# Loading two weight matrices in row groups of 2, 2, 4, 8 and 120 partitions instead of whole, in a decode kernel that streams a KV cache

## The chip, the cores and the metric

The kernel runs on one core of one Trainium2 chip. The metric is the device time of one execution in microseconds (us), lower is better. Executions of one kernel agree within about 0.25% here.

PE is the matrix engine, DVE the vector engine, ACT the scalar engine, SP the engine whose sequencer issues nearly all loads. The loads themselves are moved by 16 DMA engines, which are called "transfer engines" below. The trace shows a load as packets, which one engine moves one after another (their times are in the table below). A load has landed when all its engines have counted up its semaphore, and whoever waits for the load goes on then: in the kernel before the semaphore of the first V block has 16 arrivals, the last at 61.89 us, and PE starts on the block at 61.93 us.

## The reference

One token passes through attention over a long cache and through a gated feed-forward block, and a scalar gate mixes the two:

```python
q = (x @ wq)                                  # 32 heads of 128, x is 512 wide
scores = einsum(q, k_cache) * 128 ** -0.5     # 65,536 keys per head, bf16
a = (softmax(scores) @ v_cache) @ wo
b = (silu(x @ w_gate) * (x @ w_up)) @ w_down      # the same x
g = sigmoid((x * gate_w).sum())
return g * a + (1 - g) * b
# (cut: shapes, transposes, input setup)
```

The K and V caches have 1,074 MB together. All weights together have about 14 MB. gate and up, which the change touches, are 512 x 1792 in bf16: 1.8 MB each, 0.3% of the traffic together.

## The kernel before

On-chip memory holds three slots of 8 MB. K and V blocks of 8 MB go through them in turn. wq, gate and up share slot 0 at the start; the first K block goes to slot 1 and the first V block to slot 2. SP issues, in this order, wq, four pieces of the first K block, gate, up, the first V block. The next K block may be issued when the feed-forward matmuls have read gate and up.

```python
def dma(key, out_ap, in_ap, writes=(), reads=(), sem=None, engine="SP"):
    op(engine, key, lambda: emit[engine].dma_start(out=out_ap, in_=in_ap),
       reads=reads, writes=writes, sem=sem or key)
# ...
dma("wq", wq_sb, A_wq.rearrange("(p t) f -> p t f", t=KT), units(0, 0, WQ))
# ...
load("k", 0, [EK] * (KPP // EK))              # first K block, four pieces
G0, U0 = WQ, WQ + KT * F
gate_v, up_v = view(0, G0, KT, F), view(0, U0, KT, F)
dma("gate", gate_v, B_w_gate.rearrange("(p t) f -> p t f", t=KT), units(0, G0, U0))
dma("up", up_v, B_w_up.rearrange("(p t) f -> p t f", t=KT), units(0, U0, U0 + KT * F))
load("v", 0, [KPP])                           # first V block
# ...
def hidden():                                 # the feed-forward matmuls
    # ... 112 matmuls over gate_v and up_v
    group("gu", parts, units(0, G0, U0 + KT * F) + ["Xc"], ["m_x"])
```

Each partition receives one row of gate, 4 x 1792 x 2 = 14,336 contiguous bytes, as one packet. "Row" means this below.

The softmax here doesn't subtract the row's maximum and nothing guards it: scores larger than these inputs give would overflow.

Of the kernel before, what the change touches and what calls it, by code (L numbers as in the profile page):

```python
# [79 lines left out]
def kernel(  # L80
# [20 lines left out]
    F = B_w_gate.shape[1]  # L101
    KT = D // P
# [14 lines left out]
    def sb(name, shape, dtype):  # L117
        return consts.tile(shape, dtype, name=name)
# [11 lines left out]
    Xc = sb("Xc", [P, KT], bf16)  # L130
# [27 lines left out]
    m_x = psum.tile([P, 512], f32, name="m_x")  # L158
# [7 lines left out]
    def op(engine, key, fn, reads=(), writes=(), sem=None):  # L166
        plan.add(engine, key, fn, list(reads), list(writes), sem)

    def units(s, a, b):

        w = UNIT * Dh
        return [(s, u) for u in range(a // w, -(-b // w))]

    def view(s, a, t, n):
        return slot[s][:, a : a + t * n].rearrange("p (t n) -> p t n", t=t)

    def dma(key, out_ap, in_ap, writes=(), reads=(), sem=None, engine="SP"):
        op(
            engine, key, lambda: emit[engine].dma_start(out=out_ap, in_=in_ap),
            reads=reads, writes=writes, sem=sem or key,  # L180
        )
# [16 lines left out]
    def load(which, n, pieces):  # L198
        cache = A_k_cache if which == "k" else A_v_cache
        h, c = divmod(n, CH)  # L200
        s = where[which, n] = take()
        src = cache[0, h, c * P * KPP : (c + 1) * P * KPP, :].rearrange(
            "(p j) d -> p j d", j=KPP
        )
        t = view(s, 0, KPP, Dh)
        at = 0
        for m in pieces:
            dma(
                (which, n, at), t[:, at : at + m, :], src[:, at : at + m, :],
                units(s, at * Dh, (at + m) * Dh),  # L210
                sem=f"slot{s}" if len(pieces) == 1 else f"{which}{n}_{at}",
            )
            at += m
        assert at == KPP

    load("k", 0, [EK] * (KPP // EK))
    G0, U0 = WQ, WQ + KT * F
    gate_v, up_v = view(0, G0, KT, F), view(0, U0, KT, F)
    dma("gate", gate_v, B_w_gate.rearrange("(p t) f -> p t f", t=KT), units(0, G0, U0))
    dma("up", up_v, B_w_up.rearrange("(p t) f -> p t f", t=KT), units(0, U0, U0 + KT * F))  # L220
    load("v", 0, [KPP])


# [35 lines left out]
    def group(key, parts, reads, writes):  # L259


        def fn():
            for out_ap, pairs in parts:
                for i, (a, b) in enumerate(pairs):
                    ins = nc.tensor.matmul(  # L265
                        out_ap, lhsT=a, rhs=b, start=(i == 0), stop=(i == len(pairs) - 1)
                    )
            return ins

        op("PE", key, fn, reads, writes)  # L270

    def act(key, out_ap, in_ap, func, reads, writes, **kw):
        op(
            "ACT", key, lambda: nc.scalar.activation(out=out_ap, in_=in_ap, func=func, **kw),  # L274
            reads, writes,
        )

    def dve(key, fn, reads, writes):
        op("DVE", key, fn, reads, writes)
# [117 lines left out]
    def hidden():  # L397
        parts = []
        for w, wv in enumerate((gate_v, up_v)):
            for ft in range(FT):  # L400
                parts.append(
                    (
                        m_x[:, w * FT + ft : w * FT + ft + 1],
                        [(wv[:, t, bass.ds(ft, P, FT)], Xc[:, t : t + 1]) for t in range(KT)],
                    )
                )
        group("gu", parts, units(0, G0, U0 + KT * F) + ["Xc"], ["m_x"])
        act("gu_sb", gu_sb, m_x[:, : 2 * FT], ACT.Copy, ["m_x"], ["gu_sb"])
        act("eg", eg, gu_sb[:, :FT], ACT.Exp, ["gu_sb"], ["eg"], scale=-1.0)
        dve("eg1", lambda: nc.vector.tensor_scalar_add(eg, eg, 1.0), ["eg"], ["eg"])  # L410
        dve("eg2", lambda: nc.vector.reciprocal(eg, eg), ["eg"], ["eg"])
        dve(
            "eg3",
            lambda: nc.vector.tensor_tensor(out=eg, in0=gu_sb[:, :FT], in1=eg, op=ALU.mult),
            ["eg", "gu_sb"], ["eg"],
        )
        dve(
            "hT",
            lambda: nc.vector.tensor_tensor(out=hT, in0=eg, in1=gu_sb[:, FT:], op=ALU.mult),
            ["eg", "gu_sb"], ["hT"],  # L420
        )
# [79 lines left out]
    for n in range(N - 1):  # L501
        h, c = divmod(n, CH)
        if c == 0:
            cut[h] = len(plan.ops)
        if n:
            load("k", n, [KPP])
            load("v", n, [KPP])
        m = HK if n else EK
        for j in range(0, KPP, m):
            block(n, j, m)  # L510
            if j == 0:
                if c == 0 and h + 1 < H:
                    spread(h + 1)
                if pending:
                    diagonal()
            elif n == N - 2:
                norm(0, H - 1)
                outputs()
            while len(todo) > 1:
                gather()  # L520
        gather()
        if n == 0:
            gate()
            hidden()
        if n == N - 2:
            turn_outputs(0)
        pv(n)
# [35 lines left out]
    at = 0  # L563
# [27 lines left out]
    with tc.tile_critical():  # L591
        sems = {}
        for o in plan.ops:
            for s in [o.token[0], *o.waits]:
                if s not in sems:
                    name = "s_" + "".join(ch if ch.isalnum() else "_" for ch in str(s))
# [66 lines left out]
```

## Time and profile before

| | kernel before |
|---|---|
| time | 2522.36 us, median of 2 runs (2521.55 to 2523.16) |
| busy | PE 79%, DVE 50%, ACT 4% of the span |
| load queue | 99.7% of the span of 16 transfer engines |
| rate in the middle | 433 to 436 GB/s |
| one 65,536-byte packet | 2418 ns, the next begins about 4 ns before its end |
| one 14,336-byte packet | 535 ns, all 256 of gate and up alike |

The first view is the profile's page of the kernel before. "busy tenths" cuts the span in 40 slices; the line DMA is the busy share of the transfer engines, GB/s what they moved. The last line is the load queue: packets, bytes, share of 16 engines' span.

```profile
PE 1979.0 (79%) x9115; PEld 823.1 (33%) x9115; DVE 1268.4 (50%) x286; ACT 97.4 (4%) x398; POOL 1.9 (0%) x9
...
DMA  9999999999999999999999999999999999999998
GB/s 423 430 432 433 435 433 434 434 435 436 435 435 434 433 434 435 434 434 434 435 436 434 435 433 434 434 435 435 434 433 435 436 435 435 433 433 434 436 429 359
...
q1 hardware_dynamic: 20880, 1087.78, 99.7%
```

The transfer engines are busy all the time, the compute engines are not. The packet records of the trace say the same per engine: a 65,536-byte packet takes 2418 ns (15,959 of 16,000 to the nanosecond), so one engine moves 27.1 GB/s and 16 of them 434 GB/s. This fixed pace is the limit.

The next view lists issues: what is loaded, how often, KB each, and us from issue to landing.

```profile
slot_65<-in_B_w_gate_dram SPq DMA_DIRECT2D x1, 1792.0 KB, 34.9
slot_65<-in_B_w_up_dram SPq DMA_DIRECT2D x1, 1792.0 KB, 38.6
...
slot_67<-in_A_k_cache_dram SPq DMA_DIRECT2D x21, 35.9
```

An 8 MB block takes 19.3 us at 434 GB/s but lands 35.9 us after its issue: every engine has work queued ahead.

The chain of waits is the work that ended last, followed back from the end: start, duration, what. First its pieces near the start, then those near the end.

```profile
45.07 6.85 PE m_x L265 x112
51.92 9.96 another core or an unknown queue
61.93 16.00 PE O_ps L251 x64
77.94 41.90 DMA slot_67<-in_A_k_cache_dram
```

```profile
2390.83 13.99 PE O_ps L251 x64
...
2404.83 34.67 DMA slot_67<-in_A_k_cache_dram
...
2439.53 8.70 DVE slot_67 L324
```

At 45.07 us PE begins the 112 feed-forward matmuls; gate and up had landed at 38.4 and 42.6 us by the issues above. "another core or an unknown queue" at 51.92 is PE's wait for the first V block; the timeline names it as the load of V into slot 2 and shows PE starting on it at 61.93 us. Near the end, the last full K block lands at 2439.50 us, and some 80 us of PE and DVE work follow that hardly wait for loads any more. Therefore a microsecond added to the engine that finishes last should move the end by about a microsecond.

The last view of before divides the stretch in which gate and up are loaded into windows of 5 us. Columns: window, its length, busy us (instructions) of PE, PEld, DVE, ACT, POOL, then granted clock, DMA share and GB/s. A share over 1 shows that packets are not cut exactly at a window's edges.

```profile
core 0: us, PE busy (x) PEld busy (x) DVE busy (x) ACT busy (x) POOL busy (x), PEclk, DMA share, GB/s
33.00:38.00 5.00, 3.59 (x16) 1.49 (x16) 5.00 (x3) 0.35 (x2) 0.00 (x0) 1.00 0.99 422
38.00:43.00 5.00, 3.66 (x17) 1.49 (x16) 1.88 (x2) 0.35 (x2) 0.00 (x0) 1.00 1.20 517
43.00:48.00 5.00, 3.30 (x51) 3.25 (x52) 1.76 (x6) 0.52 (x3) 0.00 (x0) 0.76 1.12 485
48.00:53.00 5.00, 3.92 (x66) 3.84 (x64) 0.50 (x3) 0.41 (x2) 0.00 (x0) 0.50 1.02 436
```

The rate stays above 420 GB/s through all of it.

### The profile page before, as it was taken

How to read it: one execution, taken by the hardware profiler on the slowest of the kernel's cores; microseconds unless marked ns; L12 is line 12 of the kernel's file. 1: busy time of each engine (PE TensorE's matmuls, PEld its weight loads, DVE VectorE, ACT ScalarE, POOL GpSimd, SP SyncE). 2: the span in 40 equal slices, each digit the busy share in tenths (PEclk: the TensorE clock that was granted, in tenths of full speed). 3: DMA queues.
4: the chain of work that ended last, by engine and by line, in shares of the span. 5: the costliest groups of instructions: out<-in, count | busy, mean ns of one | idle time of the engine just before them, and what ended most of it. 6: DMA issues, size and time to landing. Idle time of an engine off the chain costs nothing.

```text
span 2520.2 us, 19415 instructions
## 1 busy us (share of the span) xinstructions
PE 1979.0 (79%) x9115; PEld 823.1 (33%) x9115; DVE 1268.4 (50%) x286; ACT 97.4 (4%) x398; POOL 1.9 (0%) x9
## 2 busy tenths in 40 slices
PE   4787877877778778778787787787787877877878
PEld 2233332333333333333333333333333332333334
DVE  3455355464553554644645546446455455464553
ACT  0000000000000000000000000000000000000000
POOL 0000000000000000000000000000000000000000
PEclk8888988989889899899898898998998988989888
DMA  9999999999999999999999999999999999999998
GB/s 423 430 432 433 435 433 434 434 435 436 435 435 434 433 434 435 434 434 434 435 436 434 435 433 434 434 435 435 434 433 435 436 435 435 433 433 434 436 429 359
DMA packets 20906, 1088.09 MB, mean 432 GB/s; under 512 B 2450, under 2 KB 2580, under 8 KB 2836
## 3 DMA queue, kind: packets, MB, share of 16 engines
q1 hardware_dynamic: 20880, 1087.78, 99.7%
q8 instruction: 16, 0.26, 0.0%
q14 instruction: 6, 0.05, 0.0%
q10 hardware_dynamic: 4, 0.00, 0.0%
HBM read 1087.77 MB, written 0.00 MB: 432 GB/s over the span
## 4 chain that ended last, share of the span: by engine, by line
DMA 44%; PE 41%; DVE 13%; ACT 1%; another core or an unknown queue 0%; issue 0%; SPq 0%; DVEq 0%; ACTq 0%
PE O_ps L251 18%; DMA slot_67<-in_A_k_cache_dram 16%; DMA slot_66<-in_A_k_cache_dram 14%; DMA slot_65<-in_A_k_cache_dram 14%; PE S_ps_101 L265 12%; PE S_ps_102 L265 9%; DVE slot_66 L324 4%; DVE slot_67 L324 4%; DVE slot_65 L324 3%; DVE S_sb_82 L349 2%; PE m_c L251 2%; PE m_x L265 1%; ACT P_sb_83 L274 1%; DMA slot_65<-in_A_wq_dram 0%
## 5 line engine op out<-in xcount | busy, mean ns | idle before, releaser
L265 PE MATMUL S_ps_101<-slot_67,ident 128*128 128x512 bf16 x704 | 204.1, 462 | 134.5 <-DVE slot_67 L324 134.5
L265 PE MATMUL S_ps_101<-slot_66,ident 128*128 128x512 bf16 x672 | 196.6, 464 | 128.3 <-DVE slot_66 L324 128.3
L265 PE MATMUL S_ps_101<-slot_65,ident 128*128 128x512 bf16 x672 | 189.6, 452 | 132.6 <-DVE slot_65 L324 132.6
L324 DVE TENSOR_TENSOR slot_67<-slot_67,q_bc_79 128x16384 bf16<-128x16384 bf16 (+1 forms) x26 | 207.9, 8033 | 142.0 <-DMA slot_67<-in_A_k_cache_dram 142.0
L349 DVE TENSOR_REDUCE S_sb_82<-S_ps_102 128x128 f32<-128x1024 f32 (+1 forms) x66 | 78.7, 1192 | 387.9 <-PE S_ps_102 L265 387.9
L324 DVE TENSOR_TENSOR slot_65<-slot_65,q_bc_78 128x16384 bf16<-128x16384 bf16 x22 | 190.2, 8689 | 145.7 <-DMA slot_65<-in_A_k_cache_dram 145.7
L324 DVE TENSOR_TENSOR slot_66<-slot_66,q_bc_78 128x16384 bf16<-128x16384 bf16 (+1 forms) x24 | 190.6, 7977 | 136.1 <-DMA slot_66<-in_A_k_cache_dram 120.4
L324 DVE TENSOR_TENSOR slot_67<-slot_67,q_bc_78 128x16384 bf16<-128x16384 bf16 x20 | 172.9, 8689 | 121.9 <-DMA slot_67<-in_A_k_cache_dram 121.9
L324 DVE TENSOR_TENSOR slot_66<-slot_66,q_bc_79 128x16384 bf16<-128x16384 bf16 x20 | 172.9, 8688 | 118.7 <-DMA slot_66<-in_A_k_cache_dram 118.7
L324 DVE TENSOR_TENSOR slot_65<-slot_65,q_bc_79 128x16384 bf16<-128x16384 bf16 x20 | 172.9, 8689 | 118.5 <-DMA slot_65<-in_A_k_cache_dram 118.5
L251 PE MATMUL O_ps<-slot_67,P_sb_83 128*4 128x512 bf16 x704 | 155.7, 382 | 28.3 <-ACT P_sb_83 L274 18.3
L251 PE MATMUL O_ps<-slot_65,P_sb_83 128*4 128x512 bf16 x704 | 155.2, 381 | 20.7 <-ACT P_sb_83 L274 20.7
L251 PE MATMUL O_ps<-slot_66,P_sb_84 128*4 128x512 bf16 x704 | 153.7, 379 | 19.3 <-ACT P_sb_84 L274 19.3
L265 PEld LDWEIGHTS S_ps_101<-slot_67,ident 128*128 128x128 bf16 x704 | 79.1, 115 | 258.9 <-DVE slot_67 L324 145.1
L265 PEld LDWEIGHTS S_ps_101<-slot_66,ident 128*128 128x128 bf16 x672 | 75.7, 116 | 249.1 <-DVE slot_66 L324 139.0
L265 PE MATMUL S_ps_102<-slot_67,ident 128*128 128x512 bf16 x704 | 155.9, 379 | 0.2 <-DVE slot_67 L324 0.2
L265 PEld LDWEIGHTS S_ps_101<-slot_65,ident 128*128 128x128 bf16 x672 | 74.1, 113 | 248.4 <-DVE slot_65 L324 143.2
L251 PE MATMUL O_ps<-slot_65,P_sb_84 128*4 128x512 bf16 x640 | 139.7, 379 | 18.3 <-ACT P_sb_84 L274 18.3
L251 PE MATMUL O_ps<-slot_67,P_sb_84 128*4 128x512 bf16 x640 | 139.7, 379 | 18.3 <-ACT P_sb_84 L274 18.3
L251 PE MATMUL O_ps<-slot_66,P_sb_83 128*4 128x512 bf16 x640 | 139.7, 379 | 17.5 <-ACT P_sb_83 L274 17.5
L265 PE MATMUL S_ps_102<-slot_66,ident 128*128 128x512 bf16 x672 | 148.7, 379 | 1.3 <-DVE slot_66 L324 1.3
L265 PE MATMUL S_ps_102<-slot_65,ident 128*128 128x512 bf16 x672 | 148.6, 379 | 0.1
(83 smaller groups left out, 860.1 us busy)
## 6 DMA issues: line engine op xcount, KB each, us to landing
slot_66<-in_A_k_cache_dram SPq DMA_DIRECT2D x4, 2048.0 KB, 24.7
slot_67<-in_A_k_cache_dram SPq DMA_DIRECT2D x4, 2048.0 KB, 23.9
slot_65<-in_A_wq_dram SPq DMA_DIRECT2D x1, 4096.0 KB, 12.3
slot_66<-in_A_wo_dram SPq DMA_DIRECT2D x1, 4096.0 KB, 30.7
slot_65<-in_A_v_cache_dram SPq DMA_DIRECT2D x1, 4096.0 KB, 17.6
slot_65<-in_A_v_cache_dram SPq DMA_DIRECT2D x1, 2048.0 KB, 22.1
slot_65<-in_B_w_gate_dram SPq DMA_DIRECT2D x1, 1792.0 KB, 34.9
slot_65<-in_B_w_up_dram SPq DMA_DIRECT2D x1, 1792.0 KB, 38.6
```

Source lines behind the costliest of these rows:

```text
L251: ins = nc.tensor.matmul(out_ap, lhsT=a, rhs=b, start=start and i == 0, stop=stop and i == len(pairs) - 1,)
L265: ins = nc.tensor.matmul(out_ap, lhsT=a, rhs=b, start=(i == 0), stop=(i == len(pairs) - 1))
L274: "ACT", key, lambda: nc.scalar.activation(out=out_ap, in_=in_ap, func=func, **kw),
L324: "products", lambda: nc.vector.tensor_tensor(out=w, in0=w, in1=q_rep, op=ALU.mult),
L349: lambda: nc.vector.tensor_reduce(out=S_sb[b][:, :m], in_=S_ps[r][:, :m, :], axis=AXIS.X, op=ALU.add),
```

## The change

It makes the load uneven over the transfer engines: gate is loaded as 8 and 120 rows, up as 2, 2, 4 and 120. No byte and no matmul is added. The group of matmuls waits for six loads instead of two.

```diff
-    dma("gate", gate_v, B_w_gate.rearrange("(p t) f -> p t f", t=KT), units(0, G0, U0))
-    dma("up", up_v, B_w_up.rearrange("(p t) f -> p t f", t=KT), units(0, U0, U0 + KT * F))
+    for name, w_v, w, a, b, parts in (
+        ("gate", gate_v, B_w_gate, G0, U0, [8, 120]),
+        ("up", up_v, B_w_up, U0, U0 + KT * F, [2, 2, 4, 120]),
+    ):
+        at = 0
+        for m in parts:
+            dma(
+                f"{name}{at}", w_v[at : at + m], w.rearrange("(p t) f -> p t f", t=KT)[at : at + m],
+                [(*u, name, at) for u in units(0, a, b)],
+            )
+            at += m
# ... and the group "gu" reads the names of all six pieces
```

More of the change, by code (lines that the diff above doesn't have):

```diff
@@ L406, in hidden @@
                 )
-        group("gu", parts, units(0, G0, U0 + KT * F) + ["Xc"], ["m_x"])
+        group(
+            "gu", parts,
+            units(0, G0, U0 + KT * F) + ["Xc"]
+            + [(*u, "gate", at) for u in units(0, G0, U0) for at in (0, 8)]
+            + [(*u, "up", at) for u in units(0, U0, U0 + KT * F) for at in (0, 2, 4, 8)],
+            ["m_x"],
+        )
         act("gu_sb", gu_sb, m_x[:, : 2 * FT], ACT.Copy, ["m_x"], ["gu_sb"])
```

## The prediction

> **What bounds it now.** The transfers. The page's slices show the DMA engines busy at 90% or more everywhere and some 434 GB/s; the queue table gives the load queue 99.7% of 16 engines' span for 1087.78 MB. The trace's packet records show why: every 65,536-byte packet takes 2418 ns and the next starts about 4 ns before its end, so each engine runs at a fixed 27.1 GB/s. PE is busy 79%, DVE 50%. Steady K loads are issued about 36 us before they land (DMA issues view), although 8 MB takes only 19.4 us: every engine has queued work. In the timeline the last full K load lands at 2439.5 us; some 80 us of PE and DVE work follow, with 2 to 3 us of slack against the last loads. So a microsecond added to the slowest engine's queue is a microsecond of the total.
>
> **What changes.** No byte, no matmul; two loads become six. [...] A row is 14,336 bytes, 535 ns in the trace. Rows per engine, before: 16 everywhere (8.5 us). After: engines 0 and 1 get 20, 2 and 3 get 18, 4 to 7 get 17, 8 to 14 get 16, engine 15 none. Costs:
>
> 1. Four rows more on engines 0 and 1: +2.1 us (estimate, 4 x 0.53). Engine 15's 8.5 us lead buys nothing: each slot waits for all engines. The 16 landings of one load spread over 0.7 us early and 3.4 us late, in steps of 1.2 us (single pauses of an engine), so part may hide: +1 to +2.1.
> 2. Port conflicts. [...] Likelier than not, at partial strength.
> 3. Four more issues on SP at 0.45 to 0.5 us: free, the queue is 28 us deep then. Four more waits on PE: nothing.
>
> On the critical path: 1 and 2 in full. Gate and up land at 38.4 and 42.6 us; PE uses them at 45.07, and the first V load behind them lands at 61.9. A delay to about 55 us only starts the next issue later, with the queue still full.
>
> **Predicted:** 2529 us (+7), 2522.5 to 2537. Faster by over 2%: 0.5%; within 2%: 99%; slower by over 2%: 0.5%.
>
> **What would show it.** Right: the V load's landing and every later one shift by the total's change; 14,336-byte packets take longer than 535 ns (step 2); the 16 landings of a later load spread over about 10 us, one engine far ahead (step 1); steady packets stay at 2418 ns. Step 2 wrong: those packets stay at 535 ns and the total rises 1 to 2 us.
>
> **What would make it wrong.** A different split of 120 rows [...]; the slow engines being those without extra rows (+0); a queue running dry.

The sizes of term 2: up to +4.2 us for each 120-row load (8 packets at half the pace, 8 x 0.53 us), +8.5 us for both, and +1 to +4 us for the small loads. These were estimates, on the assumption that engines which write to certain partitions at the same time share the pace of one. The sum of +7 us is +1 to +2.1 us from term 1, and the rest from term 2 taken "at partial strength"; term 3 adds nothing. The rows per engine were a forecast too; the profile after shows the counts. The packet records name no engine.

## The result, and the profile after

| | before | after |
|---|---|---|
| time | 2522.36 us (2521.55 to 2523.16) | 2534.28 us (2532.76 to 2535.79) |
| runs | 2 | 2 |
| ratio of fast runs | | 1.0047, 95% interval 1.0023 to 1.0072 |

A ratio is the mean time of one kernel's fast runs over that of the other's in the same rounds, so it is not quite the ratio of the medians quoted. The change costs 11.9 us: far less than 2%, but clear of the noise.

The page after, the same lines:

```profile
PE 1979.0 (78%) x9115; PEld 823.1 (32%) x9115; DVE 1268.2 (50%) x286; ACT 97.3 (4%) x398; POOL 1.9 (0%) x9
...
DMA  9999999999999999999999999999999999999998
GB/s 339 431 436 433 436 432 432 437 432 436 432 437 432 436 432 436 434 435 432 435 433 434 436 432 434 437 434 432 433 437 436 432 433 434 437 432 432 436 428 347
...
q1 hardware_dynamic: 20894, 1087.78, 99.6%
```

PE's busy time is the same to the last digit. The two executions that were profiled differ by 13.9 us in their spans (2520.2 to 2534.1), a little more than the medians. Of the 40 rates, the first fell from 423 to 339 GB/s, a fifth of a slice of 63 us, 12 to 13 us; the last fell from 359 to 347, the others are as before (431 to 437 in the middle). So nearly the whole cost arises in the first 63 us.

The issues after; the small groups (112, 28 and 56 KB) have no landing time in this view, so only the two large ones are shown:

```profile
slot_65<-in_B_w_gate_dram SPq DMA_DIRECT2D x1, 1680.0 KB, 41.2
slot_65<-in_B_w_up_dram SPq DMA_DIRECT2D x1, 1680.0 KB, 49.8
...
slot_67<-in_A_k_cache_dram SPq DMA_DIRECT2D x21, 36.0
```

The large part of up lands 49.8 us after its issue, where the whole of it took 38.6. A steady K block takes 36.0 against 35.9: the steady loads run as before.

The chain of waits after, near the start and near the end:

```profile
5.25 49.80 DMA slot_65<-in_B_w_up_dram
55.30 6.85 PE m_x L274 x112
62.15 12.52 another core or an unknown queue
74.71 16.67 PE O_ps L260 x64
91.40 41.17 DMA slot_67<-in_A_k_cache_dram
```

```profile
2402.56 13.99 PE O_ps L260 x64
...
2416.56 35.66 DMA slot_67<-in_A_k_cache_dram
...
2452.24 8.70 DVE slot_67 L333
```

PE now waits for up until 55.05 us. It starts on the first V block 12.8 us later than before (74.71 against 61.93), and the last full K block lands 12.7 us later (2452.22 against 2439.50). The tail behind it is the same work (1.2 us longer in this execution, 0.7 of it in one group of PE matmuls). So the delay of the first stage arrives at the end almost whole: 12.7 of the 13.9 us between these two executions.

The same windows after:

```profile
core 0: us, PE busy (x) PEld busy (x) DVE busy (x) ACT busy (x) POOL busy (x), PEclk, DMA share, GB/s
33.00:38.00 5.00, 3.39 (x17) 1.47 (x16) 3.72 (x3) 0.35 (x2) 0.00 (x0) 1.00 0.98 200
38.00:43.00 5.00, 2.32 (x12) 0.97 (x11) 3.52 (x2) 0.35 (x2) 0.00 (x0) 1.00 0.90 181
43.00:48.00 5.00, 1.98 (x10) 0.81 (x8) 1.75 (x6) 0.52 (x3) 0.00 (x0) 1.00 1.02 222
48.00:53.00 5.00, 0.00 (x0) 0.00 (x0) 0.00 (x0) 0.00 (x0) 0.00 (x0) 0.65 1.28 284
```

While gate and up are loaded the rate falls to 181 to 222 GB/s, half of before, and the transfer engines count as busy all the time: they are not idle, they are slow. The packet records show it directly. They name no engine; I linked each packet to the one that starts within nanoseconds of its end, which gives one row per engine (a few links are uncertain). The numbers are ns per 14,336-byte packet, in order:

```
before, any engine, 16 packets:   535 535 535 535 535 535 535 535 535 535 535 535 535 535 535 535
after, engine with 20 packets:    1484 1055 1089 1135 1079 1125 1107 1135 1104 1040 1009 1119 980 952 1185 1179 1136 1049 1047 964
after, engine with 16 packets:    1411 1113 1076 1126 1081 1121 1108 1125 1089 1059 1004 1138 994 946 1152 1193
after, another engine with 16:    1574 1032 1104 1138 1073 1514 1595 1620 1224 1151 1052 942 1100 1501 1607 1626
after, engine with none, first V packets (65,536 bytes, 2418 before):   5285 6614 4904 6021
```

The unevenness is as predicted: some engines have 20 rows, some 18, some 17, some 16, one none. In the trace, the semaphores of the groups of 8, 2, 2 and 4 rows have 9, 3, 3 and 5 arrivals: one at the issue (at 4.0 to 5.4 us, long before the first of these rows moves at 31.8 us), then 8, 2, 2 and 4, as many as there are rows. That of a 120-row group has 16: one at the issue and 15. This fits 8, 2, 2, 4 and 15 engines.

But two things go beyond the prediction. Every engine with rows is slowed to about half (0.93 to 1.3 us for most packets, 535 ns before); this trace alone does not say whether an engine is slowed only by those that write to certain partitions or by any. And the engine that has no row of gate or up, and so began on V early, needs 4.9 to 6.6 us for packets that take 2.4.

Two engines take 1.5 to 1.64 us for two or three packets in a row from 38 us on, and again from 48 us on (one of the two is printed, in the fourth row of numbers). In this time the engine without rows is writing V. Of the packets of the other engines between 38 and 41.5 us, none takes more than 1,139 ns. So whatever slowed these two further did not slow the others; why it was these two is not shown.

### The profile page after: what moved, and what is told of

It is laid out like the page before. It is cut to its first block, busy times and chain, and to the rows that moved or that the text cites. A ratio compares the mean times of both kernels' runs of the same rounds, so it can differ in the third digit from the quotient of the medians.

```text
span 2534.1 us, 19421 instructions
## 1 busy us (share of the span) xinstructions
PE 1979.0 (78%) x9115; PEld 823.1 (32%) x9115; DVE 1268.2 (50%) x286; ACT 97.3 (4%) x398; POOL 1.9 (0%) x9
## 4 chain that ended last, share of the span: by engine, by line
DMA 46%; PE 40%; DVE 12%; ACT 1%; another core or an unknown queue 0%; issue 0%; SPq 0%; DVEq 0%
PE O_ps L260 18%; DMA slot_67<-in_A_k_cache_dram 16%; DMA slot_65<-in_A_k_cache_dram 14%; DMA slot_66<-in_A_k_cache_dram 14%; PE S_ps_101 L274 12%; PE S_ps_102 L274 9%; DVE slot_67 L333 4%; DVE slot_65 L333 3%; DVE slot_66 L333 3%; DMA slot_65<-in_B_w_up_dram 2%; DVE S_sb_82 L358 2%; PE m_c L260 1%; PE m_x L274 1%; ACT P_sb_83 L283 1%
```

## The experiments

Theories, as they stood:

- **Rows.** The fullest engine has 4 rows more, 4 x 0.53 = 2.1 us, and everybody waits for it.
- **Ports.** "Port" is whatever engines share that write to neighbouring partitions at the same time. Two such engines would take about twice 535 ns for a packet, four about four times (estimates, by an even share); the theory took two for 64-row loads and four for 16-row loads. Loads over all 128 partitions would stay as they are (535 ns in the kernel before). In the prediction only the engines that crowd each other were slow. No trace had shown this when the expectations were written.
- **Rivals.** A fixed cost for each load; a weakness of loads that use fewer than 16 engines; a slow reading side (neighbouring rows in memory).

Every kernel below gave the right result and was timed in 5 rounds beside the kernel before, whose medians were 2522.49, 2522.60 and 2522.97 us in the three groups. Differences are those of medians.

### Even, on part of the partitions: two loads of 64 rows, eight loads of 16

```diff
-        ("gate", gate_v, B_w_gate, G0, U0, [8, 120]),
-        ("up", up_v, B_w_up, U0, U0 + KT * F, [2, 2, 4, 120]),
+        ("gate", gate_v, B_w_gate, G0, U0, [64, 64]),             # second kernel: [16] * 8
+        ("up", up_v, B_w_up, U0, U0 + KT * F, [64, 64]),          # second kernel: [16] * 8
```

> Gate and up each as two loads of 64 rows: all 16 engines get the same number of rows (4 per load, 16 in all)[...]. Port theory: 14,336-byte packets about 1,050 ns instead of 535, first V load about 8.4 us later, total +8.4 us (2530.8), landings of a V load as close together as before (under 1 us). Uneven-load theory (only the extra rows of the fullest engine cost): no engine has more rows, so +0. Theory that groups of fewer than 16 engines or odd group sizes are slow: +0.[...]

> Gate and up each as eight loads of 16 rows, one row per engine and load: even again[...]. Port theory: packets about 2,100 ns, total +25 us (2547.7). Uneven-load theory: +0. Theory that each additional load costs a fixed time (14 more loads here, 4 more in the change and +11.9 us there): +42 us.

With 64-row loads: 2531.46 us (+9.0, as the port theory expected with +8.4), ratio 1.0037 (1.0023 to 1.0051). With 16-row loads: 2540.48 us (+18.0), ratio 1.0072 (1.0058 to 1.0085). The windows of the two, 64 rows first:

```profile
core 0: us, PE busy (x) PEld busy (x) DVE busy (x) ACT busy (x) POOL busy (x), PEclk, DMA share, GB/s
33.00:38.00 5.00, 3.63 (x16) 1.49 (x16) 3.70 (x3) 0.35 (x2) 0.00 (x0) 1.00 0.98 210
38.00:43.00 5.00, 2.79 (x9) 1.11 (x10) 2.76 (x2) 0.35 (x2) 0.00 (x0) 0.82 1.03 218
```

```profile
core 0: us, PE busy (x) PEld busy (x) DVE busy (x) ACT busy (x) POOL busy (x), PEclk, DMA share, GB/s
33.00:38.00 5.00, 3.57 (x16) 1.47 (x16) 2.30 (x3) 0.35 (x2) 0.00 (x0) 1.00 0.98 132
38.00:43.00 5.00, 0.90 (x4) 0.30 (x4) 4.70 (x2) 0.27 (x2) 0.00 (x0) 0.90 1.02 138
```

All 16 engines are at work at about one pace in both (the DMA share, taken over 16 engines, is 0.98 to 1.03; 16 packets of 14,336 bytes in 1,667 ns are 137.6 GB/s), so they have about the same bytes. Still the rate is 210 to 218 GB/s and 132 to 138 GB/s. Nearly all packets take 0.9 to 1.15 us with 64 rows (1,134 where they are longest and steady), and about 1,667 ns with 16 rows. So unevenness is not needed for the loss, nor is a load on fewer engines. 16 packets of 1.667 us against 0.532 are 18.2 us; the loss measured is 18.0.

The size for 16 rows was missed: 2,100 ns and +25 us were expected, by the estimate of four times 535 ns. A possible reason is that the engines are a little apart in time, so that fewer than four crowd each other at once; that is argued only, and not shown.

### The same bytes to other partitions

Rows 0 to 63 of gate in eight loads of 8 rows; rows 64 to 127 in one load; up whole. The twin reads the same source rows in the same order on the same engines, but writes them to partitions 4 apart. So that the result stays right, it permutes x for these rows.

```diff
+            o = w_v[at : at + m]                 # first kernel: 8 neighbouring partitions
+            if m == 8:                           # twin: 8 partitions, 4 apart
+                p = at // 32 * 32 + at % 32 // 8
+                o = w_v[p : p + 29 : 4]
+            dma(f"{name}{at}", o, w.rearrange("(p t) f -> p t f", t=KT)[at : at + m], names)
# the twin's gate matmuls use a copy of x in the order of those partitions
```

> Only gate changed: rows 0 to 63 as eight loads of 8 neighbouring rows (engines 0 to 7[...]), rows 64 to 127 as one load; up whole. Uneven by 4 rows on engines 0 to 7 (and those have 4 rows of the 64-row load as everyone). Port theory: packets of the 8-row loads about 2,100 ns, total about +17 us. Uneven-load theory alone: 4 to 8 rows more on engines 0 to 7, +2 to +4 us.

> The same loads as the run with 8 neighbouring rows: same source rows in the same order, same engines, same bytes; but the 8 rows go to partitions 4 apart[...] (x is permuted to match, the result stays right). Port theory: packets of the 8-row loads about 535 ns, those of the 64-row load about 1,050; total about +4 us, some 13 us less than its twin. Theory that the reading side (neighbouring rows in memory) or the number of engines per load slows the packets: the same time as its twin.

Neighbouring partitions: 2536.20 us (+13.7), ratio 1.0055 (1.0042 to 1.0069). Partitions 4 apart: 2531.00 us (+8.5), ratio 1.0034 (1.0020 to 1.0048). The same reads, 5.2 us apart (more than the runs of either spread: 2535.72 to 2536.93 against 2530.04 to 2532.81). Where the bytes are written decides; a slow reading side and a fixed cost per load are out as the explanation of this gap.

The sizes were missed (+17 and +4 us were expected), and the packets say where (ns, one engine per row; the first group has packets of the 8-row loads, the others start with the 64-row load):

```
neighbouring, engine with 8-row loads:   535 1729 1676 1680 1680 1678 1668 1691 | 1671 1798 1821 1704 | 1222 549 539 535 535 535 535 535
neighbouring, engine without:            1167 1673 1698 1692 | 1680 1678 1686 1685 1774 1807 1684 1272
4 apart, engine with 8-row loads:        535 812 1047 1109 1074 739 636 601 | 731 1692 1834 1665 | 1484 572 535 539 535 535 535 535
4 apart, engine without:                 535 974 1086 1112 | 966 702 604 604 1035 1818 1794 1684
```

The engines without 8-row loads begin with the 64-row load, which goes to the upper 64 partitions, while the 8-row loads go to the lower 64. They are slowed exactly like the others: 1.68 us. (Their own 64-row load may have a part in it: in the twin, with the 8-row loads 4 apart, its first packets take up to 1.1 us.) In the twin the slow packets come in the time when some engines are in the 64-row load, and then they come for everybody. This does not fit the prediction's form, in which only the engines that crowd each other are slow. It suggests what is called a jam below: engines that write to neighbouring partitions slow all 16. The next group tests this.

### Rows alone, and a jam made on purpose

The kernel before, gate and up whole, with additional loads of 57,344 bytes per partition (4 rows' worth) ahead of gate. They go to slot 2, which the first V block overwrites; V waits for them. Four kernels: one such load on engines 0 and 1, four of them, and a pair of twins with two loads on engines 0 to 3.

```diff
+    for i in range(2):                       # engines 0 to 3; the other two: p=2, range(1) or range(4)
+        dma(
+            f"more{i}", slot[2][i : i + 13 : 4, : 4 * KT * F],        # apart: partitions 0, 4, 8, 12
+            # beside: slot[2][4 * i : 4 * i + 4, ...]                 #   partitions 0, 1, 2, 3
+            A_k_cache[0, 5 + i, : 16 * KT * F // Dh, :].rearrange("(p j) d -> p (j d)", p=4),
+            [("more", i)],
+        )
     dma("gate", ...)
     dma("up", ...)
+    op("SP", "more_in", None, reads=[("more", i) for i in range(2)])
     load("v", 0, [KPP])
```

> The kernel before with one load more: 57,344 bytes (four rows' worth) on each of engines 0 and 1 alone, into partitions 0 and 4[...]. The unevenness of the change without its port conflicts. Term 1 of the prediction: +1 to +2.1 us, the 14,336-byte packets of gate and up stay at 535 ns, two engines land late. If unevenness itself costs what the change cost: +12.

> Four times that, on the same two engines: 229,376 bytes each. If the fullest engine sets the time, 16 rows x 0.53 = +8.4 us, less at most 1.2; if other engines could take up the slack, or the queue's slack hid it, less than half of that.

> The kernel before with two loads more of 57,344 bytes on each of engines 0 to 3, into partitions 4 apart [...]: +4.2 us, gate and up packets stay at 535 ns.

> The same two loads (same source, bytes, engines) into partitions 0 to 3 and 4 to 7[...]. Port theory in the prediction's form (only the engines on the crowded port are slowed): engines 0 to 3 need 13 to 17 us instead of 4.2, total +13 to +17, while gate and up packets of the other twelve engines stay at 535 ns[...]. Theory of a jam[...]: gate and up packets of all other engines also take 1,600 ns or so as long as the four are at work, total again +13 to +17.

| run | more on the fullest engine | at 0.53 us a row | time | difference | ratio (95%) |
|---|---|---|---|---|---|
| 2 engines, 1 load | 4 rows | 2.1 | 2523.01 | +0.4 | 1.0001 (0.9987 to 1.0014) |
| 4 engines, 2 loads, apart | 8 rows | 4.2 | 2525.12 | +2.5 | 1.0007 (0.9993 to 1.0021) |
| 2 engines, 4 loads | 16 rows | 8.5 | 2529.05 | +6.5 | 1.0024 (1.0010 to 1.0037) |
| 4 engines, 2 loads, beside | 8 rows | 4.2 | 2536.50 | +13.9 | 1.0056 (1.0042 to 1.0070) |

The first three rows, all below what was expected, lie on one line: the rows' time less 1.7 to 2.0 us. The fullest engine sets the pace, but the first 1.7 us or so seem free. Each interval is some 3 us wide to either side, and the first two differences are within the noise. The traces show the same without that noise: the last engine's landing of the first V block moves from 61.89 us before to 62.47, 64.75 and 68.66, that is by 0.6, 2.9 and 6.8 us for 2.1, 4.2 and 8.5 us of additional work. The slack is seen there too: in the kernel before, 14 engines have landed this block by 60.63 us and two at 61.87 and 61.89, so most engines can take 1.3 us more before anyone waits for them. By the last full K block the 16 landings are spread from 2436.32 to 2439.50 us.

The second and the last row are twins: the same source, bytes and engines. Only the partitions differ, and beside costs 11.4 us more than apart. The chain of waits of the two, first apart, then beside; "in_A_v_cache_dram" is the wait for the first V block and the line below it PE's start on it:

```profile
37.02 27.73 DMA slot<-in_A_v_cache_dram
64.79 15.77 PE O_ps L258 x64
```

```profile
49.82 27.34 DMA slot<-in_A_v_cache_dram
77.21 15.78 PE O_ps L258 x64
```

The start on V moves from 64.79 to 77.21 us. The packets of gate and up on an engine that has nothing to do with the additional loads (ns):

```
apart:    535 535 535 535 535 535 535 535 535 535 535 535 535 535 535 535
beside:   535 1802 2211 2211 1845 1059 2194 2194 2188 932 565 535 535 535 535 535
```

Here gate and up are whole, as in the kernel before and in the twin, where their packets take 535 ns; only the additional loads, by forecast on engines 0 to 3, go to four neighbouring partitions. Yet all the others, too, take up to 2.2 us for a packet (2,194 to 2,252 ns where it is steady): 4.1 to 4.2 times 535 ns, more than the 1.6 us that the jam theory expected. They do so twice, once for each of the two loads, and when the second is done they are at 535 ns again. This is the jam, and it decides against the prediction's form of the theory: the packets of the other twelve engines did not stay at 535 ns. The total time could not have decided it: the four engines' own additional packets took 6.9 to 8.4 us each instead of 2.1, which makes their two loads 10 to 12 us longer and by itself can account for the 11.4 us. That the destination makes the jam is shown by the twins; where on the way it sits is not shown.

### The two halves of the change, and the number of loads

```diff
 # gate alone                                     # up alone
-    ("gate", ..., [8, 120]), ("up", ..., [2, 2, 4, 120])
+    ("gate", ..., [8, 120]), ("up", ..., [128])  # ("gate", ..., [128]), ("up", ..., [2, 2, 4, 120])
 # eight loads over all 128 partitions: four column groups of each
+        for t in range(KT):
+            dma(f"{name}{t}", w_v[:, t], w.rearrange("(p t) f -> p t f", t=KT)[:, t], names)
```

> Only gate is split (8 and 120 rows), up stays whole. Jam theory: the eight 14,336-byte packets per engine of the 120-row load take about 1,090 ns instead of 535 on every engine (+4.5 us), the 8-row load holds everybody for about 1.1 us more; the extra row on engines 0 to 7 hides in the 1.8 us that were free in the runs with more rows. Total +5 to +6 us. If the jam came from up's small groups alone: about +0.

> Only up is split (2, 2, 4 and 120 rows), gate stays whole. Jam theory: +4.5 us for the 120-row load and 1.5 to 3 for the three small ones on engines 0 to 3, less what hides: +5 to +7 us. With the run that splits gate alone it should add up to the whole change's 11.9 within 2 us.

> Gate and up each as four loads (by quarter of a row, 3,584-byte packets), but every load over all 128 partitions: two loads more than in the change[...], no uneven engine. If the number of loads, their issues on SP or the additional semaphore waits cost anything: up to +12. Jam theory: +0 [...].

Gate alone: 2529.03 us (+6.1), ratio 1.0026 (1.0012 to 1.0039). Up alone: 2529.32 us (+6.3), ratio 1.0028 (1.0014 to 1.0041). Together 12.4, against 11.9 for the whole change: the halves add up. With up alone the eight packets of gate, which is whole, take 535 ns, and those of up mostly 0.9 to 1.2 us: the slowness comes with the split loads and not before them.

Eight loads by columns: 2522.13 us (-0.8), ratio 1.0000 (0.9987 to 1.0014). All 1,024 packets take 140 ns. Two loads more than in the change, and no cost. The number of loads, their issues and the additional waits are out. The issues were hidden, not free: in SP's timeline the four issues of up take 22.26 us, where the one issue of the kernel before took 0.49, and the first V block was issued at 27.89 us instead of 4.50. Its turn on the transfer engines came only at some 41 us, so nothing waited for it.

No version beats the kernel before: the best, the split by columns, is the same within the noise.

## Why the prediction was right or wrong

The prediction said 2529 us, with 2522.5 to 2537 as the range; 2534.28 was measured. The range holds and the direction is right. The increase is 11.9 us instead of 7, and both terms of the sum were mis-sized, in opposite directions. Taken at full strength, the prediction's own terms make +11.6 to +14.6 us (2.1 + 8.5 + 1 to 4; the last two are the estimates told beside the prediction); its middle was pulled down to +7 by the guess that the conflicts would come "at partial strength".

- **What bounds the kernel: right.** The added time went from the first V block (12.8 us later) to the last full K block (12.7 us later) to the end (13.9 us in these two executions, 11.9 us by medians).
- **Term 1, "four rows more on engines 0 and 1: +2.1 us", of which it left +1 to +2.1: too large.** Measured with loads to partitions 4 apart, four rows cost 0.4 us in time (within the noise) and 0.6 us at the landing of the first V block; with eight and sixteen, 1.4 to 1.7 us of the fullest engine's work hid there. That "part may hide" was said; most of it hid.
- **"Engine 15's 8.5 us lead buys nothing": right in effect, and even the lead shrank.** The engine without rows needed 4.9 to 6.6 us for each of its first four V packets. It landed the first V block at 65.01 us, the next engine at 71.79, the last at 74.67, and PE started on the block at 74.71.
- **Term 2, port conflicts: that the place written to slows the packets was right, strength and reach were not.** Up to +8.5 us (its size, above) "at partial strength" became full strength: most packets took 0.93 to 1.3 us instead of 535 ns. The reach: engines that have no part in the crowded loads can be slowed as well, as the other twelve were in the run "beside" (2,194 to 2,252 ns). Whether the cost of the change itself needs the jam is not shown. The sum can be checked on an engine with 20 rows: its 20 packets span 21.80 us (32.17 to 53.97) where 16 took 8.52 before. That is +13.3; its first V packet adds 0.36 (2773 ns instead of 2418). Of these 13.6 us, 12.8 arrive at the last landing of the first V block; the rest hid there. The medians cannot check it more closely: the interval of the 11.9 us is 5.8 to 18.2.
- **Term 3, issues and waits free: right.** Eight loads by columns cost nothing. The next K block was issued at 62.18 us, before any engine had finished the first V block, so no engine ran out of work.
- **Signs.** Packets over 535 ns: seen. Landings of a later load spread over about 10 us, one engine far ahead: 9.66 us for the first V block. Steady packets at 2418 ns: seen.

What stays open: how the rows of a load are dealt to the engines; why the first packets of the 64-row load took up to 1,130 ns in the twin with partitions 4 apart; why four neighbouring partitions make 2.2 us per packet with long loads, but 16-row and 8-row loads only 1.67 to 1.68 us; why four engines on neighbouring partitions slow all the others, and what slowed two engines further in the change itself did not; and which partitions, besides neighbouring ones, get into each other's way (of small loads to other partitions, only 4 apart was tested).

## What to carry to other kernels

When a load must be cut, cut it along the free dimension and keep all 128 partitions: eight column groups cost nothing here (their issues were hidden: the first V block was issued at 27.89 us and its turn came at some 41 us), while cuts by rows cost 6 to 18 us on at most 3.7 MB. A load into a few neighbouring partitions does not only run slowly itself; it can slow loads that go elsewhere: four engines on four neighbouring partitions made the packets of the other twelve four times as long (2,194 to 2,252 ns for 535), for as long as they were at work. So in this kernel, which is bound by its transfers, the cost of such a load follows from how long the jam lasts, and not from how few bytes it moves. Uneven bytes per engine cost here only what the fullest engine has beyond a slack of 1.7 to 2.0 us (+0.4, +2.5 and +6.5 us for 2.1, 4.2 and 8.5 us of additional work); read packet durations before blaming the byte counts.
